# A written-out instruction order, and the engine of some casts and squares, replaced in a fused recurrence and MLP kernel

## The chip, the cores and the metric

The kernel runs on one core of a Trainium2 chip. Its time is the device time of one launch in microseconds; a kernel is told by the median over its runs. A profile is one further execution, taken by the hardware profiler, with a time of its own. TensorE is written PE, VectorE DVE, ScalarE ACT, GpSimd POOL and SyncE SP, as in the profile.

## What is computed

The first part is a linear recurrence over 768 steps for 4 batches and 8 heads of 48; the second is a two-layer MLP on its output.

```python
batch, n_heads, seq, head_dim = (4, 8, 768, 48)
n_tokens, d_model, d_ff = (3072, 384, 2048)
for t in range(S):
    cur = np.einsum('bhd,bhe->bhde', u[None] * kt, vt)
    y[:, :, t] = np.einsum('bhd,bhde->bhe', rt, state + cur)
    state = wt[:, :, :, None] * state + np.einsum('bhd,bhe->bhde', kt, vt)
x = attn_out.transpose(0, 2, 1, 3).reshape(B * S, H * D)
h = x @ w_in
r = np.maximum(h, 0.0)
g = s * (r * r) + b
return g @ w_out
```

## The kernel before

The recurrence is cut into 24 chunks of 128 time steps, numbered by `n`. A chunk has one operation of each of these names, most of them a single instruction or one group of matmuls. `load n.0` to `n.3` bring w, r, k and v (192 KB each; for chunks 0 to 3, two chunks are loaded together, 384 KB). `ln` takes the logarithm of w on ACT (line 317). `cum` sums it along time with triangular matrices on PE (L372, L391, with small column sums L380, L397); `exp` on ACT (L413), `inc` on DVE (L418) and `exn` on ACT (L428) turn the sums into decay factors, and `mul` on DVE (L437, L444) multiplies r and k by them. `tr` transposes both on PE (L471) and `tev` copies the result on ACT (L491, L494); from chunk 9 on, `tev` is a transposing DMA on SP's queue instead (L501). `mt` is the chunk's attention matrix on PE for a pair of chunks (L531, L543), `msk` its mask on DVE (two per chunk, L555), `vb` a cast of v to bf16 (L870 on ACT, L872 on POOL). `dmm` (L625, L638), `sup` (DVE, L671, L679) and `st` (POOL, L688) with `l2` (POOL, L458) carry the state to the next chunk of the same batch. `rkp`, `rku`, `yd` on POOL (L322, L328, L351) and `cd` on DVE (L345) make the term with u, which `u_mm` and `u_ev` (L893, L897) spread over the partitions. `ymm` gives the chunk's output on PE (L574, L586, L597, L606), `yev` takes it out on DVE (L651), `xtr` transposes it on PE (L699) and `xev` puts it into the MLP's input on ACT (L714).

The MLP works on 12 tiles `T` of two chunks, 256 tokens. `g1 T.i` (i = 0 to 7) is six matmuls of the first layer (L749), `relu T.i` its ACT pass (L762), `sq T.i` the square, on ACT (L772) or DVE (L774). `g2 T.q` is four matmuls of the second layer (L793): q = 0 to 3 for the tile's first 128 tokens, 4 to 7 for the other 128; the last tile has its second 128 tokens in two halves of the columns, 4 to 7 and 8 to 11. `oev T.k` scales and adds on DVE (L804), `store T.k` is the DMA to the output (L823). In the names of the order the tile's number and i or q are written together: `g211.4` is `g2` of tile 11, q = 4.

Early in the kernel `li0` to `li3` and `lo0` to `lo3` load the two weight matrices in pieces of 768 KB, `ci` and `co` cast them to bf16, and `csred`, `csadd`, `cssplit` (DVE), `csspread` (PE, L849) and `csevac` (ACT, L855) make the constant row that b and the column sums of `w_out` give. `small` and `small2` load s and b. `warm` matmuls (L1119, written `+16`) only use PE while it has nothing else.

No scheduler runs when the kernel is built. The order is written out by hand as one text, `ORDER`; each engine and each DMA queue gets its operations in the sequence in which the text names them, `@A`, `@D` or `@P` gives the engine where there is a choice, and every queue works strictly in that order. Waits come from data and from buffers that are used in a ring: an operation that takes a buffer must wait until its user of one round before is done.

```python
need = o["deps"] + o["after"]
for tag, last in o["takes"]:
    h = held[tag]
    if len(h) >= self.rings[tag]:
        need += h[-self.rings[tag]]
    h.append(last)
```

The rings that matter here are six PSUM banks `P` for nearly all PE results but those of `g2`, two PSUM banks `o` for `g2`, eight r/k buffers, five for w, six for v, four for the output rows and four for the weight pieces. The numbers in the `add(...)` calls are the planner's costs and due times from which an order was searched beforehand; they issue no instruction.

Of the kernel before, what the change touches and what calls it, by code (L numbers as in the profile page):

```python
# [38 lines left out]
load0.0 load0.1 load_u ln0 ln1 +16 cum0.0 cum0.1 cum1.0 exp0.0 load0.2 exp0.1 mul0.0 mul0.1 exp1.0  # L39
load0.3 mul1.0 cum1.1 load2.0 load2.2 load2.3 u_mm tr0 exp1.1 mul1.1 +2 tr1 u_ev tev0 tev1 +9 mt0  # L40
vb0@P load4.0 l20 rkp0 rku0 load2.1 rkp1 l21 msk0.0 msk1.0 vb1@A ln2 msk0.1 rku1 li0 ln3 cd0 +4
cum2.0 exp2.0 dmm0 cum3.0 msk1.1 cum3.1 ln4 vb2@A cum2.1 sup0 exp3.0 exp2.1 vb3@A st0 +1 cum4.0 li1
exp3.1 l22 yd0 mul2.0 mul2.1 exp4.0 mul3.0 ymm0 cd1 mul3.1 yd1 ymm1 dmm1 tr2 sup1 rkp2 l23 ci0@A
yev0 dmm2 tev2 tr3 li2 rku2 sup2 yev1 xtr0 tev3 cd2 +5 xtr1 l24 rkp3 xev0 rku3 yd2 xev1 +1 mt2 g10.0
ci1@A msk2.0 st2 msk2.1 msk3.0 li3 g10.1 relu0.1 msk3.1 relu0.0 dmm3 g10.2 g10.3 relu0.2 lo0 ymm2
ci2@D cd3 ymm3 lo1 st1 yd3 lo2 sup3 yev2 cum4.1 xtr2 ci3@A relu0.3 g10.4 load5.0 sq0.0@D lo3 load5.1
yev3 load6.0 load4.1 sq0.3@A g10.5 co0@D load4.2 xev2 xtr3 load5.2 csred0@D sq0.2@A sq0.1@A relu0.4
g10.6 xev3 exp4.1 small2 g20.4 g20.0 g10.7 load4.3 g11.0 g11.1 co1@D relu0.5 g11.2 sq0.5@A relu0.7
relu0.6 sq0.4@D sq0.7@A csred1@D sq0.6@A ln5 small g11.3 relu1.0 vb4@P load5.3 rkp4 csadd1@D relu1.2
relu1.3 g20.1 g11.4 cum5.0 relu1.1 exp5.0 co2@D csred2@D g20.5 cum5.1 exp5.1 sq1.2@A csadd2@D  # L50
# [113 lines left out]
def kernel(  # L164
# [15 lines left out]
    B, H, S, D = r.shape  # L180
# [979 lines left out]
```

## Time and profile before

| | us |
|---|---|
| median of 11 runs | 186.07 |
| lowest, highest run | 185.84, 189.53 |
| profiled execution, its own time | 186.16 |
| span of the profiled execution | 184.1 |
| PE, DVE, ACT, POOL busy | 176.5, 140.6, 146.5, 106.3 |
| `g1` and `g2` matmuls, busy (L749, L793) | 71.9, 72.7 |

The span runs from the first to the last instruction; 2.06 us of the profiled run's time lie outside it. A group's busy time is the time in which at least one of its instructions was running; since matmuls overlap, the mean of one is longer than its share. "Idle before" names the instruction whose end let the engine go on. A row of busy time by stage gives the stage, its length, the busy time of PE, PE's weight loads, DVE, ACT and POOL with the number of instructions in brackets, the granted share of PE's clock, the mean busy share of the DMA engines and the rate in GB/s.

### The profile page before, as it was taken

Reading aid. Unit: us, or ns where it says so; the run is one execution under the profiler, and the core shown is the slowest. Engines: PE = TensorE matmul, PEld = TensorE weight load, DVE = VectorE, ACT = ScalarE, POOL = GpSimd, SP = SyncE. Lnnn points to the kernel's source line nnn. Section 1 sums busy time; section 2 is a strip of 40 time slices with the busy share of each in tenths; the row PEclk is TensorE's granted clock in tenths of the full one; section 3 lists DMA queues with packets and bytes.
Section 4 is the critical chain, followed back from the end, with each engine's and each line's share of the span. In section 5 each row is a group of like instructions: output and inputs, shape, how many; then the busy total and the mean of one; then the engine's idle time right before and its main releaser. Section 6 shows DMA issues by size and latency. Waiting matters only on the chain.

```text
span 184.1 us, 5087 instructions
## 1 busy us (share of the span) xinstructions
PE 176.5 (96%) x1994; PEld 139.6 (76%) x1994; DVE 140.6 (76%) x250; ACT 146.5 (80%) x286; POOL 106.3 (58%) x139
## 2 busy tenths in 40 slices
PE   7999999998999999997999999999999999999993
PEld 4468898865797787785788878877886978888672
DVE  7659899999969878959978698697898959522231
ACT  3589999997889999888878979878989687754900
POOL 3684950049698999698397199195396493100000
PEclk9999999999999999999999999999999999999999
DMA  6999999879999769898799989999874890004022
GB/s 160 325 327 365 393 317 318 165 139 221 208 192 220 182 123 217 179 212 183 134 221 185 177 197 218 215 238 200 193 162 97 193 192 4 2 5 171 0 85 85
DMA packets 113449, 34.14 MB, mean 185 GB/s; under 512 B 108177, under 2 KB 111378, under 8 KB 113426
## 3 DMA queue, kind: packets, MB, share of 16 engines
q1 hardware_dynamic: 113426, 33.83, 79.3%
q8 instruction: 15, 0.25, 0.5%
q14 instruction: 8, 0.07, 0.1%
HBM read 25.17 MB, written 4.72 MB: 162 GB/s over the span
## 4 chain that ended last, share of the span: by engine, by line
PE 46%; ACT 3%; DVE 2%; issue 0%; ACTq 0%
PE o_ps L793 21%; PE h_ps L749 19%; PE mt_ps L543 2%; DVE mt_sb L555 2%; PE y_ps L606 1%; ACT rh L762 1%; PE xt_ps L699 1%; PE y_ps L597 1%; ACT gT L772 1%; PE d_ps L638 1%; PE cums L391 1%; DVE o_sb L804 1%; ACT E L428 0%; ACT xT L714 0%; DVE inc L418 0%; ACT E L413 0%
## 5 line engine op out<-in xcount | busy, mean ns | idle before, releaser
L793 PE MATMUL o_ps<-w_out,gT 128*128 128x384 bf16 (+1 forms) x400 | 72.7, 320 | 1.0 <-DVE o_sb L804 0.7
L749 PE MATMUL h_ps<-xT,w_in 128*128 128x256 bf16 x576 | 71.9, 273 | 0.2
L762 ACT ACTIVATE rh<-h_ps 128x512 bf16<-128x512 f32 x96 | 55.3, 601 | 13.9 <-PE h_ps L749 12.8
L749 PEld LDWEIGHTS <-w_in 128*128 128x128 bf16 x576 | 61.7, 114 | 4.3 <-issue 0.2
L793 PEld LDWEIGHTS <-gT 128*128 128x128 bf16 x400 | 36.5, 98 | 18.6 <-DVE gT L774 0.8
L772 ACT ACTIVATE gT<-rh 128x512 bf16<-128x512 bf16 x69 | 42.5, 636 | 0.3
L351 POOL TENSOR_TENSOR yd<-vt,cd 128x384 bf16<-128x384 f32 x20 | 19.0, 954 | 18.4 <-DVE cd L345 18.4
L555 DVE TENSOR_TENSOR mt_sb<-mt_ps,tri_strict 128x512 bf16<-128x512 f32 x40 | 25.4, 681 | 2.7 <-PE mt_ps L543 2.7
L328 POOL TENSOR_TENSOR rku<-rkp,u_bc 128x384 f32<-128x384 f32 x24 | 25.3, 1057 | 0.7
L322 POOL TENSOR_TENSOR rkp<-rkt 128x384 f32<-128x384 f32 x20 | 23.7, 1189 | 1.3 <-DMA rkt<-in_k_dram 1.3
L804 DVE SCALAR_TENSOR_TENSOR o_sb<-o_ps,s_bc,bconst 128x384 f32<-128x384 f32 (+1 forms) x25 | 14.8, 594 | 11.8 <-PE o_ps L793 11.8
L444 DVE TENSOR_TENSOR prd<-rkt,E 128x768 bf16<-128x768 f32 x20 | 23.2, 1164 | 0.5 <-ACT E L428 0.3
L774 DVE TENSOR_TENSOR gT<-rh 128x512 bf16<-128x512 bf16 x27 | 14.9, 562 | 9.2 <-ACT rh L762 9.1
L413 ACT ACTIVATE E<-cums 128x388 f32<-128x388 f32 (+1 forms) x32 | 15.8, 497 | 6.5 <-DVE inc L418 3.2
L688 POOL TENSOR_TENSOR st<-stmp,l 128x384 bf16<-128x384 bf16 x16 | 16.4, 1026 | 6.4 <-DVE stmp L679 6.4
L872 POOL CAST vb<-vt 128x384 bf16<-128x384 f32 x12 | 7.2, 603 | 16.1 <-DMA vt<-in_v_dram 16.1
L651 DVE TENSOR_TENSOR x_sb<-y_ps,yd 128x384 bf16<-128x384 f32 x24 | 13.0, 553 | 4.2 <-PE y_ps L606 2.2
L345 DVE TENSOR_REDUCE cd<-rku 128x8 f32<-128x384 f32 x24 | 12.9, 543 | 0.6 <-POOL rku L328 0.6
L714 ACT COPY xT<-xt_ps 128x384 bf16<-128x384 bf16 x24 | 11.0, 487 | 2.5 <-PE xt_ps L699 2.4
L418 DVE TENSOR_TENSOR inc<-cums,logw 128x384 f32<-128x384 f32 x16 | 8.8, 550 | 3.9 <-ACT E L413 3.4
L317 ACT ACTIVATE logw<-wt 128x384 bf16<-128x384 f32 x20 | 10.6, 531 | 0.0
L679 DVE TENSOR_TENSOR stmp<-d_ps,st 128x384 bf16<-128x384 f32 x16 | 8.7, 551 | 2.1 <-PE d_ps L638 2.0
(94 smaller groups left out, 199.4 us busy)
## 6 DMA issues: line engine op xcount, KB each, us to landing
out_dram<-o_sb SPq DMA_DIRECT2D x23, 192.0 KB, 3.3
wt<-in_w_dram SPq DMA_DIRECT2D x20, 192.0 KB, 3.9
rkt<-in_r_dram SPq DMA_DIRECT2D x20, 192.0 KB, 4.0
rkt<-in_k_dram SPq DMA_DIRECT2D x20, 192.0 KB, 3.8
vt<-in_v_dram SPq DMA_DIRECT2D x20, 192.0 KB, 3.6
wi_st<-in_moe_w_in_dram SPq DMA_DIRECT2D x4, 768.0 KB, 9.1
wo_st<-in_moe_w_out_dram SPq DMA_DIRECT2D x4, 768.0 KB, 5.8
pkt<-in_w_dram SPq DMA_DIRECT2D x2, 384.0 KB, 4.1
```

What stands on the lines that cost most here:

```text
L322: nc.gpsimd.tensor_tensor(out=rkp, in0=c["r"], in1=c["k"], op=ALU.mult)
L328: nc.gpsimd.tensor_tensor(out=rku.rearrange("t h d -> t (h d)"), in0=c["rkp"].rearrange("t h d -> t (h d)"), in1=u_bc, op=ALU.mult,)
L351: nc.gpsimd.tensor_tensor(out=yd, in0=c["v"], in1=c["cd"].unsqueeze(2).to_broadcast([128, H, D]), op=ALU.mult,)
L413: nc.scalar.activation(out=c["E"][:, x, 0:w], in_=ps[:, 0:w], func=AF.Exp)
L444: nc.vector.tensor_tensor(out=prd[:, :, :, 0:D], in0=c["rk"], in1=c["E"][:, :, 0:HD].rearrange("t x (h d) -> t x h d", h=H), op=ALU.mult,)
L555: nc.vector.tensor_tensor(out=c["mt"][:, sg], in0=c["mt_ps"][sg], in1=(masks[:, n % 2] if packed(n) else tri_strict) .unsqueeze(1) .to_bro ...
L688: nc.gpsimd.tensor_tensor(out=c["st_new"], in0=c["stmp"].rearrange("q p (g e) -> q p g e", g=2), in1=c["l2"].unsqueeze(3).to_broadcast([12 ...
L749: nc.tensor.matmul(ps[:, f, :], lhsT=w_in_sb[ft // FPP][:, kt, :].rearrange("p (m j) -> p j m", j=FPP)[:, ft % FPP, :], rhs=xT[T][:, kt, : ...
L762: nc.scalar.activation(out=rh, in_=hs[T, i], func=AF.Relu)
L772: nc.scalar.activation(out=g, in_=rh, func=AF.Square)
L793: nc.tensor.matmul(os_[T, k][:, cols], lhsT=gT[T][:, ft, tt * 128 : (tt + 1) * 128], rhs=w_out_sb[ft // FPP][:, ft % FPP, cols], start=(ft ...
L804: nc.vector.scalar_tensor_tensor(out=o_sb[:, cols], in0=os_.pop((T, k))[:, cols], scalar=s_bc, in1=bconst[:, cols], op0=ALU.mult, op1=ALU.add,
```

## The change

The text `ORDER` is replaced by another one of the same 1105 words, found by a search that took the mean over seven sets of disturbed durations. Nothing else that issues an instruction is different: the operations, the buffers and their rings, and the 38 warm-up matmuls are the same. The engines of ten casts of v and of 23 squares are exchanged; 11 casts are on ACT and 13 on POOL in both, 69 squares are on ACT before and 68 after. One of the planner's costs, that of `u_mm`, is 0.85 instead of 0.7. The diff is cut to the beginning, up to the first groups of tile 2, two later stretches and the end:

```diff
--- before
+++ after
 ORDER = """
-load0.0 load0.1 load_u ln0 ln1 +16 cum0.0 cum0.1 cum1.0 exp0.0 load0.2 exp0.1 mul0.0 mul0.1 exp1.0
-load0.3 mul1.0 cum1.1 load2.0 load2.2 load2.3 u_mm tr0 exp1.1 mul1.1 +2 tr1 u_ev tev0 tev1 +9 mt0
-vb0@P load4.0 l20 rkp0 rku0 load2.1 rkp1 l21 msk0.0 msk1.0 vb1@A ln2 msk0.1 rku1 li0 ln3 cd0 +4
-cum2.0 exp2.0 dmm0 cum3.0 msk1.1 cum3.1 ln4 vb2@A cum2.1 sup0 exp3.0 exp2.1 vb3@A st0 +1 cum4.0 li1
-exp3.1 l22 yd0 mul2.0 mul2.1 exp4.0 mul3.0 ymm0 cd1 mul3.1 yd1 ymm1 dmm1 tr2 sup1 rkp2 l23 ci0@A
-yev0 dmm2 tev2 tr3 li2 rku2 sup2 yev1 xtr0 tev3 cd2 +5 xtr1 l24 rkp3 xev0 rku3 yd2 xev1 +1 mt2 g10.0
-ci1@A msk2.0 st2 msk2.1 msk3.0 li3 g10.1 relu0.1 msk3.1 relu0.0 dmm3 g10.2 g10.3 relu0.2 lo0 ymm2
-ci2@D cd3 ymm3 lo1 st1 yd3 lo2 sup3 yev2 cum4.1 xtr2 ci3@A relu0.3 g10.4 load5.0 sq0.0@D lo3 load5.1
-yev3 load6.0 load4.1 sq0.3@A g10.5 co0@D load4.2 xev2 xtr3 load5.2 csred0@D sq0.2@A sq0.1@A relu0.4
-g10.6 xev3 exp4.1 small2 g20.4 g20.0 g10.7 load4.3 g11.0 g11.1 co1@D relu0.5 g11.2 sq0.5@A relu0.7
-relu0.6 sq0.4@D sq0.7@A csred1@D sq0.6@A ln5 small g11.3 relu1.0 vb4@P load5.3 rkp4 csadd1@D relu1.2
-relu1.3 g20.1 g11.4 cum5.0 relu1.1 exp5.0 co2@D csred2@D g20.5 cum5.1 exp5.1 sq1.2@A csadd2@D
-load6.1 load6.2 g11.5 co3@D sq1.0@D g11.6 csred3@D csadd3@D load7.0 cssplit g11.7 g20.2 g20.6 g20.3
-rku4 mul4 relu1.4 load8.0 sq1.3@A ln6 load9.0 relu1.6 relu1.7 sq1.1@A cum6.1 g20.7 relu1.5 csspread
-load6.3 mul5 tr4 cum6.0 load7.1 tr5 csevac sq1.5@A l25 oev0.1 oev0.0 exp6.0 tev5 exp6.1 dmm4 g21.4
-g21.0 tev4 g21.1 g21.5 vb5@P sup4 sq1.4@A cd4 dmm5 mul6 mt4 rkp5 load7.2 ln7 load7.3 g21.6 sup5
-msk4.0 msk5.0 sq1.6@A sq1.7@A cum7.0 rku5 st5 l26 ln8 exp7.0 msk4.1 tr6 g21.2 yd4 tev6 load10.0
-load8.3 cd5 cum7.1 yd5 ymm4 msk5.1 g21.7 st4 yev4 load8.1 ln9 vb6@P exp7.1 load8.2 ymm5 yev5 cum8.0
-inc8 xtr4 mul7 load9.1 load9.3 cum9.0 xev4 dmm6 xtr5 st3 g21.3 l27 xev5 exp8.0 load11.0 vb7@P g12.0
-rkp7 sup6 exn8 load10.1 g12.1 inc9 exp9.0 oev1.1 relu2.0 sq2.0@A g12.2 relu2.1 dmm7 tr7 rku7 g12.3
-tev7 relu2.2 rkp6 sq2.1@D oev1.0 load11.3 vb8@P cd7 sup7 mul8 load9.2 g12.4 g22.0 relu2.3 relu2.4
...
-g14.1 g14.2 g14.3 cd10 relu4.0 exp13.0 inc13 sup11 mul12 l212 cd11 oev3.0 relu4.1 yd10 vb12@P mt10
-relu4.2 g14.4 g23.7 relu4.3 sq4.0@D sq4.1@A load13.3 load14.1 exn13 st10 load13.2 msk10.0 msk11.0
-load15.0 oev3.1 rkp12 l213 msk10.1 relu4.4 ln14 g14.5 store2.0 load16.0 g24.4 st11 msk11.1 sq4.2@A
-cum14.0 g24.0 dmm12 rku12 sq4.4@A g14.6 yd11 sup12 mul13 ymm10 ymm11 yev10 ln15 rkp13 relu4.5
...
-relu7.7 sq7.7@A store5.1 relu8.0 mt18 tev20 exn21 msk19.0 relu8.1 msk18.0 msk18.1 yd19 g27.6 g18.2
-ln22 msk19.1 g18.3 cum22.0 dmm18 g27.2 sq8.1@A ln23 inc22 mul21 g27.3 ymm19 g18.4 g27.7 relu8.3
-relu8.2 rkp20 sq8.0@A load22.2 g18.5 tev21 sq8.3@A yev19 relu8.4 exp22.0 rku20 yd18 vb21@P rkp21
-sup18 relu8.5 ymm18 xtr19 rku21 st18 sq8.2@A exn22 cum23.0 sq8.4@D g18.6 oev7.1 yev18 oev7.0 xtr18
-g18.7 g28.0 inc23 store7.0 relu8.6 g28.4 load20.3 g28.5 cd21 xev18 exp23.0 xev19 supn21 supn20
-sq8.5@A relu8.7 load23.2 mt20 store6.1 g19.0 mul22 g19.1 g28.1 msk20.0 msk20.1 msk21.0 yd21 msk21.1
...
-xev23 relu10.6 relu10.7 oev9.0 sq10.4@D g111.0 g111.1 g29.7 g111.2 sq10.5@D relu11.1 g210.4 sq10.7@A
-g111.3 g111.4 relu11.0 g111.5 oev9.1 sq10.6@D sq11.1@D g111.6 relu11.5 g111.7 relu11.2 sq11.5@A
-relu11.3 sq11.2@A sq11.0@A relu11.6 store9.1 g210.5 relu11.7 g210.0 g210.6 g210.7 store8.1 store9.0
-g210.1 relu11.4 sq11.3@A g210.2 store8.0 sq11.6@D sq11.7@D oev10.1 g210.3 sq11.4@D g211.8 g211.0
-g211.1 oev10.0 store10.1 g211.2 g211.4 g211.3 g211.5 g211.6 g211.7 g211.9 g211.10 g211.11 oev11.0
-oev11.1 oev11.2 store10.0 store11.1 store11.0 store11.2
-"""
+load0.0 ln0 load0.2 load0.1 ln1 +17 cum0.0 cum0.1 exp0.0 mul0.0 cum1.0 cum1.1 exp0.1 exp1.0 mul0.1
++3 tr0 load0.3 l21 exp1.1 mul1.0 mul1.1 vb0@A l20 vb1@A load_u u_mm rkp0 tr1 dmm0 u_ev load2.0
+load4.0 tev0 tev1 sup0 ln2 rku0 load2.1 st0 cd0 rkp1 ln3 +5 mt0 +1 cum2.0 cum2.1 load2.3 load2.2
+msk0.0 li0 cum3.0 ln4 vb3@A msk1.0 exp2.0 vb2@A msk0.1 li2 +1 cum4.0 exp3.0 msk1.1 yd0 mul2.0 cum3.1
+rku1 exp2.1 exp3.1 mul2.1 cd1 l22 mul3.0 ymm0 ci0@A ymm1 li1 yev0 exp4.0 tr2 dmm1 yd1 mul3.1 +8 xtr0
+rkp3 li3 tev2 yev1 rku3 sup1 xev0 st1 tr3 rkp2 ci2@D xtr1 xev1 dmm2 sup2 lo0 tev3 load5.0 +3 g10.0
+ci1@A mt2 msk3.0 relu0.0 lo1 g10.1 g10.2 msk2.0 msk2.1 sq0.0@A relu0.1 msk3.1 rku2 ci3@A g10.3 g10.4
+st2 relu0.4 relu0.2 l23 l24 ymm3 cd3 sq0.1@D yd3 ymm2 lo2 cd2 lo3 yev3 xtr3 small2 yd2 co0@D g10.5
+relu0.3 sq0.2@A sq0.4@A ln5 yev2 relu0.5 g10.6 xtr2 g20.4 xev2 csred0@D xev3 load6.0 load4.1 load4.2
+load5.1 sq0.3@A load5.2 relu0.6 cum5.0 g10.7 co1@D sq0.5@A load6.1 csred1@D csadd1@D co2@D g11.0
+g20.0 relu0.7 exp5.0 sq0.7@A relu1.0 g11.1 csred2@D cum5.1 exp5.1 sq0.6@A g20.1 g11.2 g11.3 cum4.1
+g20.5 co3@D small relu1.3 relu1.2 relu1.1 sq1.0@A load7.0 csadd2@D load6.2 ln6 load4.3 load5.3 g20.6
+g11.4 csred3@D g11.5 relu1.4 g20.2 exp4.1 csadd3@D load6.3 sq1.3@A g20.3 cum6.0 relu1.5 g20.7
+cssplit sq1.1@A mul4 csspread sq1.2@D csevac g11.6 exp6.0 relu1.6 cum6.1 mul5 tr4 dmm3 exp6.1 l26
+g11.7 tev4 tr5 oev0.1 tev5 sup3 relu1.7 sq1.4@A oev0.0 g21.0 g21.1 rkp4 mt4 rkp5 g21.4 vb4@P mul6
+msk5.0 sq1.5@A sq1.7@A rku4 rku5 msk4.0 load8.0 l25 msk4.1 tr6 cd4 dmm4 load9.0 sup4 yd4 load7.1 st4
+load7.2 sq1.6@A vb5@A cd5 ln7 vb6@A tev6 load7.3 msk5.1 load8.1 ln8 g21.5 g21.2 g21.6 load8.2 dmm5
+cum7.0 exp7.0 yd5 ymm4 g21.7 sup5 yev4 ymm5 cum7.1 xtr4 cum8.0 yev5 inc8 load9.3 load10.0 load9.1
+ln9 dmm6 rkp6 st3 l27 exp7.1 load11.0 load8.3 xev4 vb7@P xtr5 xev5 cum9.0 exp8.0 mul7 load9.2 sup6
+g21.3 exn8 g12.0 exp9.0 g12.1 rkp7 rku6 relu2.0 tr7 g12.2 relu2.1 inc9 st5 oev1.1 oev1.0 sq2.1@A
+rku7 g12.3 dmm7 tev7 relu2.2 sq2.0@D relu2.3 g12.4 sup7 mul8 cd6 rkp8 relu2.4 g12.5 g22.4 mt6
...
+g23.2 dmm10 cd10 g14.0 sup10 exn12 relu4.0 rku11 load13.3 mt10 g23.6 g14.1 sq3.7@A msk10.0 msk10.1
+msk11.0 cum13.0 g14.2 g14.3 store1.1 load13.1 msk11.1 inc13 mul12 cd11 load13.2 load14.0 relu4.1
+ymm10 relu4.2 sq4.0@D exp13.0 rkp12 store2.1 relu4.3 exn13 g23.3 g23.7 yd10 load16.0 load15.0
+load14.1 sq4.1@A ymm11 g14.4 load14.3 oev3.1 yd11 rkp13 g24.0 g14.5 st11 rku12 g14.6 load14.2
+sq4.2@A sq4.3@A ln14 relu4.4 load15.1 l212 relu4.5 mul13 relu4.6 yev11 load12.3 oev3.0 yev10 rku13
...
+sq8.6@A mt18 g28.2 g28.4 yd19 g28.5 load21.3 msk19.0 load22.1 msk19.1 msk18.0 sq8.7@A exn22 rkp21
+store6.1 ymm19 g28.6 cum23.0 exp23.0 rku21 load22.2 msk18.1 yev19 ymm18 cd21 xtr19 yev18 rku20 inc23
+g28.3 xtr18 g28.7 vb20@P xev18 xev19 mt20 supn20 cd20 msk20.0 g19.0 g19.1 vb21@P yd20 msk20.1 g19.2
...
+g210.3 g111.4 relu11.2 relu11.3 g111.5 g111.6 sq11.1@D sq11.0@D sq11.2@D oev10.0 relu11.5 g111.7
+relu11.4 sq11.4@A sq11.3@D relu11.7 g210.7 relu11.6 g211.0 g211.1 sq11.7@D sq11.6@D oev10.1 sq11.5@A
+g211.8 g211.4 store10.0 g211.5 store10.1 g211.2 g211.9 g211.3 g211.6 oev11.0 g211.7 oev11.1 g211.10
+store11.0 g211.11 oev11.2 store11.1 store11.2
 """
...
 add("load_u", "SP", 0.5, load_u, (), [], [], U_AT, dma=0.1)
-add("u_mm", "PE", 0.7, spread_u, (), ["load_u"], [("o", ["u_ev"])], 2.0, lat=0.2)
+add("u_mm", "PE", 0.85, spread_u, (), ["load_u"], [("o", ["u_ev"])], 2.0, lat=0.2)
 add("u_ev", "DVE", 0.45, u_evac, (), ["u_mm"], [], 2.0)
```

## The prediction

> **What bounds the kernel now.** I read the page first, then busy time by stage, then the waits of TensorE and ScalarE, then TensorE's timeline where it waits.
>
> ```profile
> span 184.1 us, 5087 instructions
> PE 176.5 (96%) x1994; PEld 139.6 (76%) x1994; DVE 140.6 (76%) x250; ACT 146.5 (80%) x286; POOL 106.3 (58%) x139
> PEclk9999999999999999999999999999999999999999
> ```
>
> TensorE (PE) is busy in 96% of the span and its clock is granted throughout, so what an order can save is TensorE idle time and slack at the two ends. By stage (us, then busy us of PE, PEld, DVE, ACT, POOL):
>
> ```profile
> 0.00:21.00 21.00, 19.12 (x292) 13.26 (x293) 15.41 (x41) 15.00 (x26) 13.55 (x33) 1.00 1.00 308
> 21.00:51.80 30.80, 29.65 (x352) 23.48 (x352) 29.31 (x46) 28.09 (x52) 15.13 (x18) 1.00 0.98 237
> 51.80:170.00 118.20, 116.81 (x1269) 95.11 (x1268) 92.06 (x157) 98.42 (x201) 77.64 (x90) 1.00 0.79 165
> ```
>
> The reader sees three regimes. Up to 21 us the pipeline fills. From 21 to 51.8 three engines are nearly full at once: PE idles 1.15, DVE 1.49, ACT 2.71 us. From there to 170 us PE idles only 118.20 - 116.81 = 1.39 us. TensorE's waits, first for 20 to 52 us, then for 52 to 181 us:
>
> ```profile
> PE trps L471 <- DVE prd L444: 1.2, 2, 0.8
> ```
>
> ```profile
> PE o_ps L793 <- DVE o_sb L804: 0.7, 1, 0.7
> PE o_ps L793 <- DVE gT L774: 0.3, 1, 0.3
> PE xt_ps L699 <- ACT E L428: 0.3, 1, 0.3
> ```
>
> The timeline places them: both transposes of chunks 4 and 5 late behind `mul4`, `mul5`; `g24.4` and `g24.0` late behind a DVE burst of masks; one `xtr` late behind an exponential.
>
> ```profile
> 41.01 0.62 PE L471 MATMUL trps<-identity,prd 128*128 128x128 bf16 x8 [0.34 <-DVE prd L444]
> 42.68 0.62 PE L471 MATMUL trps<-identity,prd 128*128 128x128 bf16 x8 [0.81 <-DVE prd L444]
> 84.30 0.82 PE L793 MATMUL o_ps<-w_out,gT 128*128 128x384 bf16 x4 [0.33 <-DVE gT L774]
> 86.02 0.81 PE L793 MATMUL o_ps<-w_out,gT 128*128 128x384 bf16 x4 [0.66 <-DVE o_sb L804]
> 139.78 0.34 PE L699 MATMUL xt_ps<-identity,x_sb 128*128 128x128 bf16 x3 [0.32 <-ACT E L428]
> ```
>
> A rule weighed here: the Trainium skill, "Perfetto Trace Analysis", section "Identifying the Most-Contended Engine", says that matmul busy share is no measure of headroom and to judge by weight-load busy share and MFU. By weight loads, 95.11 of 118.20 us, the long stage would have 23 us of room. The rows say otherwise for an order: in the chain six `g1` matmuls take 0.66 us and four `g2` matmuls 0.65, group after group, 109 and 163 ns each with no gap. I take the row: 1.4 us of room there, not 23.
>
> **The change, part by part.** No instruction is added or dropped on TensorE (3987 rows each, 38 warm-up matmuls in both). `u_mm` 0.7 to 0.85 is a planner's number that issues nothing: 0. The 24 casts of v stay 11 on ACT and 13 on POOL, with other members, and of 96 squares 68 instead of 69 are on ACT. One square is 0.52 us of ACT (two back to back, 1.15 us busy and the next begins 1.04 after) and about 0.4 of DVE; both have over 35 us idle in the span, so the totals are 0. What counts is where each queue's work stands. I compare at points where TensorE has issued the same set of work in both orders, so that its time is directly comparable. Two exist early: the end of `tr5` (43.14 us before) and the start of `g12.0` (51.79).
>
> Start to `g10.0` (20.94 before). `vb0` goes from POOL to ACT and stands with `vb1` ahead of `tev0`. ACT waits 0.90 us there before, and two casts of 0.43 fill it; `mt0` stays at 11.1. `dmm0` and `sup0` move ahead of the masks, and `u_mm` (0.85) behind `tr0`, covered by `tev0`. The four masks then end near 14.1 and `ymm0` starts there, not at 15.1. But `g10.0` also waits for `ci0` (its 768 KB load stands behind the same loads as before) and for `xev1`: 16.5 + 1.4 cast, 0.4 `exp4.0`, 0.95 `tev2`, 0.8 two `xev` = 20.1. `tev3` (0.95) and then `mt2` come after it, not before it. Gain 0.8, returned by `mt2`: 21.7 after `mt2` and `g10.0` against 21.6. Sum 0.
>
> To `tr5`. Before, `tr4` follows `csspread` at once and waits out `mul4`, `mul5` (1.46 us each, DVE rows from 39.69 to 42.62). After, `g11.6`, `cum6.1` (0.66 + 0.16) stand between `csspread` and `tr4`, and `dmm3`, `g11.7` (0.44 + 0.66) between `tr4` and `tr5`: 1.9 us of work in front of the wait. But DVE has done less: up to `cssplit` it drops three squares and `sup3` and takes one square, 1.2 us less, while PE up to `csspread` does 1.7 us less. So half a microsecond of the cover is spent on `csspread` itself. On POOL, `rkp4`, `rkp5` now precede `vb4`, whose load 4.3 falls from sixteenth to twentieth on SP's queue from `li0` on, past 6.1, 7.0, 6.2 and the slow 512 B load `small` (2.20 us on SP). It is issued near 39.5 instead of 35.15 (2.2, and three loads of about 0.7) and lands 3.6 later, near 43; `dmm4`, its first user, comes near 45, so 0, but a further 2 us would reach TensorE.
>
> The second rule: "GPSIMD Engine Reference" (its opening table, SBUF interfaces) says that POOL shares them with VectorE and that DVE instructions with two SBUF inputs contend. That speaks against this move, because `rkp4`, `rkp5` now run beside `csred3`, `csadd3`. The rows agree on size: `rkp` takes 1.71 us beside `mul4`, 1.00 alone, and `mul` 1.46 against 0.95. By the rule alone `tr5` loses about 0.5; but POOL then sits waiting for load 4.3 while `mul4`, `mul5` run, and they lose 2 x 0.5. Net DVE: `cssplit` 39.7, `mul4` 40.65, square 41.05, `mul5` 42.0, `tr5` ends 42.6 at best and 43.0 if the muls keep 1.46. I take a gain of 0.3 of the 1.15.
>
> To `g12.0`. ACT must finish `xev5`. Its queue up to there gains `vb0`, `vb5`, `vb6` (3 x 0.43) and `sq0.0`, `sq0.4`, `sq1.0` (3 x 0.52) and loses `sq0.1`, `sq1.2` (2 x 0.52): +1.8 us. These are its waits from 16 to 52 us:
>
> ```profile
> ACT RK L494 <- PE trps L471: 0.9, 1, 0.9
> ACT xT L714 <- PE xt_ps L699: 0.5, 1, 0.5
> ACT bconst L855 <- PE csb_ps L849: 0.3, 1, 0.3
> ACT rh L762 <- PE h_ps L749: 0.2, 1, 0.2
> ```
>
> With 0.2 more and the 0.90 before `tev0`, 3.0 us are there to fill. From `tev5` (end 43.6 to 44.0) 7.4 us of queue follow to `xev5`, with 0.3 of small waits 51.3 to 51.7. TensorE, at the same work, would arrive at 51.5. So `g12.0` gains 0.3; bounds +1.8 (nothing filled) and -0.7.
>
> 51.8 us to the end. Of 1.39 us idle, 0.99 is at `g24.4` and `g24.0`. Before, 2.8 us of PE work lie between `mt10` and `g24.0`; after, 5.6 (`g23.6`, `g14.1`, `g14.2`, `g14.3`, `ymm10`, `g23.3`, `g23.7`, `ymm11`, `g14.4`, `cum13.0`). DVE must by then do four masks, `inc13`, `mul12`, `cd11`, one square, `oev3.1`: 4 x 0.61 + 0.47 + 0.95 + 0.47 + 0.41 + 0.53 = 5.3. So 0.9 to 0.6 of it goes. The 0.32 at `xtr18` goes with its neighbours. What is late next: `ymm18` 3.1 us behind `mt18` (four masks, 2.5), and `mt20`, `g19.0` behind `inc23` and `xev19` with a few tenths of cover. I give new waits 0.8 in all, from 0.3 to 2.0, for 118 us that I can't follow wait by wait; the old order has 1.39. The tail does not move: both orders end in two half groups of 0.33, the 0.42 `o_sb` and a store.
>
> Sum: 0 - 0.3 - 1.4 + 0.8 = -0.9. The profiled run took 186.16 with a span of 184.1; the median shown is 186.07. Span 183.2, time 185.2.
>
> **The rivals.**
> 1. ACT turns late (slower). Place: `g12.0` behind `xev5`. ACT has 1.8 us more to do by then and runs full for 28 us in a row. It decides once ACT idles over about 1 us between `relu0.0` and `xev5`, by a late `ci1`, `ci3`, `tr5` or load 4.3. If the cover is gone, +1.8, then -1.4 and the same mechanism's later waits of +0.9: 187.4. For it: ACT already has 28.09 of 30.80 us busy. Against: each old wait is one that the new order puts work into.
> 2. Waits only change places (no change): no gain at `g12.0`, 1.4 of new waits for 1.4 old: 186.1. For it: every wait of the long stage is under 0.7 us, so small misplacements make as many.
> 3. Everything is covered: -0.7 at `g12.0` and 0.3 of new waits for 1.4: 184.3. Against: the masks of `mt18` and `mt20`.
>
> **How the numbers follow.** Likeliest case (185.2, own range 184.7 to 185.5) 0.33, rival 3 0.09, rival 2 0.23, rival 1 0.35. A measurement of this kernel tells about 0.3%, 0.56 us, from no change. Faster 0.42, same 0.23, slower 0.35. Range 184.0 (rival 3's lower side) to 188.2 (rival 1 with 2 instead of 0.9 of later waits, less its tail).
>
> **What would show it.** Right: `tr4`, `tr5` with under 0.6 us of wait together; `g12.0` near 51.5; ACT nearly without waits from 22 to 51; under 0.5 us at `g24.0`; long-stage PE idle under 1 us. Wrong: PE waiting for ACT's `xT` at `g12.0`; `dmm4` waiting for `vb4`; TensorE idle over 1.5 us after 52, above all near `mt18` to `g19.0`, or a transpose on SP late ahead of an `mt`.

## Result, and the profile after

| | before | after |
|---|---|---|
| median, us | 186.18 (48 runs) | 184.05 (13 runs) |
| ratio of comparable runs | | 0.9899, 95% interval 0.9877 to 0.9920 |
| profiled execution, its own time, us | 186.16 | 183.94 |
| span, us | 184.1 | 182.2 |

Medians are of all runs; ratios leave out runs more than 1.5% above the fastest of the same kernel. The change makes the kernel 1% faster: 2.1 us in the median where 0.9 was predicted. The time lies in the range given (184.0 to 188.2), but below the own range of the likeliest case (184.7 to 185.5). It is what rival 3, "everything is covered", stood for (184.3).

The page after. TensorE has the same busy time in a shorter span:

```profile
span 182.2 us, 5106 instructions
PE 176.5 (97%) x1994; PEld 139.8 (77%) x1994; DVE 144.2 (79%) x251; ACT 145.5 (80%) x285; POOL 103.8 (57%) x139
```

Busy time by stage, the columns as before (length, then busy PE, PEld, DVE, ACT, POOL; clock; DMA share; GB/s):

```profile
0.00:21.00 21.00, 19.39 (x264) 13.26 (x265) 15.78 (x40) 15.03 (x26) 14.10 (x31) 1.00 0.99 301
21.00:51.80 30.80, 30.66 (x387) 24.09 (x386) 28.99 (x47) 29.93 (x57) 14.29 (x20) 1.00 0.99 249
51.80:170.00 118.20, 117.83 (x1273) 95.38 (x1271) 95.63 (x159) 97.32 (x197) 75.43 (x90) 1.00 0.81 164
```

TensorE's idle time fell from 1.15 to 30.80 - 30.66 = 0.14 us in the second stage and from 1.39 to 118.20 - 117.83 = 0.37 in the third. ACT went from 28.09 to 29.93 busy of 30.80: the 1.8 us of casts and squares that the new order gives it went into its old idle time.

TensorE's waits from 52 us on were three lines, 1.3 us in all. Now there is one:

```profile
PE xt_ps L699 <- DVE x_sb L651: 0.3, 1, 0.3
```

TensorE's timeline, the rows that answer to the late transposes of before and the start of `g12.0`. None of them has a releaser behind it, so none waits:

```profile
40.36 0.61 PE L471 MATMUL trps<-identity,prd 128*128 128x128 bf16 x8
42.03 0.61 PE L471 MATMUL trps<-identity,prd 128*128 128x128 bf16 x8
51.11 1.47 PE L749 MATMUL h_ps<-xT,w_in 128*128 128x256 bf16 x12
```

The points at which both orders have issued the same set of TensorE work place the gain (us; each is the start of what follows, the 115th operation is taken 0.65 us behind the start of its last group, and TensorE's end is the end of its last row):

| point | before | after | difference |
|---|---|---|---|
| end of `mt2` and `g10.0` | 21.60 | 21.85 | +0.25 |
| end of `tr5` | 43.14 | 42.47 | -0.67 |
| start of `g12.0` | 51.79 | 51.11 | -0.68 |
| 115th operation (`g22.3` after, `g13.5` before) | 70.08 | 69.15 | -0.93 |
| end of TensorE | 180.87 | 178.66 | -2.21 |

These are one profile of each kernel. A second profile of the kernel after (`after_again`, below) has 21.95, 42.71, 51.34 and 178.92 at four of these points, so a difference is good to some 0.3 us. 0.3 us is given back behind TensorE, in the last `o_sb` and stores (3.5 us from TensorE's end to the end of the span, 3.2 before), and the time outside the span is 1.74 instead of 2.06.

### The profile page after: what moved, and what is told of

It is laid out like the page before. It is cut to its first block, busy times and chain, and to the rows that moved or that the text cites. A ratio compares the mean times of both kernels' runs of the same rounds, so it can differ in the third digit from the quotient of the medians.

```text
span 182.2 us, 5106 instructions
## 1 busy us (share of the span) xinstructions
PE 176.5 (97%) x1994; PEld 139.8 (77%) x1994; DVE 144.2 (79%) x251; ACT 145.5 (80%) x285; POOL 103.8 (57%) x139
## 4 chain that ended last, share of the span: by engine, by line
PE 84%; SPq 6%; DMA 5%; DVE 2%; ACT 1%; issue 1%; DVEq 0%
PE o_ps L793 34%; PE h_ps L749 33%; DMA wi_st<-in_moe_w_in_dram 5%; SPq L304 4%; PE mt_ps L543 3%; PE y_ps L606 2%; PE xt_ps L699 2%; PE cums L391 2%; PE y_ps L597 2%; PE d_ps L638 2%; PE trps L471 1%; SPq L719 1%; DVE prd L444 1%; ACT w_in L870 1%; PE y_ps L586 1%
## 5 line engine op out<-in xcount | busy, mean ns | idle before, releaser
L749 PE MATMUL h_ps<-xT,w_in 128*128 128x256 bf16 x576 | 72.9, 273 | 0.1
L762 ACT ACTIVATE rh<-h_ps 128x512 bf16<-128x512 f32 x96 | 54.8, 601 | 15.1 <-PE h_ps L749 14.4
L772 ACT ACTIVATE gT<-rh 128x512 bf16<-128x512 bf16 x68 | 41.5, 639 | 0.3
L351 POOL TENSOR_TENSOR yd<-vt,cd 128x384 bf16<-128x384 f32 x20 | 17.7, 886 | 24.1 <-DVE cd L345 17.5
L774 DVE TENSOR_TENSOR gT<-rh 128x512 bf16<-128x512 bf16 x28 | 15.7, 575 | 12.1 <-ACT rh L762 12.0
L444 DVE TENSOR_TENSOR prd<-rkt,E 128x768 bf16<-128x768 f32 x20 | 24.1, 1208 | 0.1
L322 POOL TENSOR_TENSOR rkp<-rkt 128x384 f32<-128x384 f32 x20 | 21.0, 1054 | 1.9 <-DMA rkt<-in_k_dram 1.9
L458 POOL TENSOR_TENSOR l<-E,par 128x8 f32<-128x8 f32 x20 | 6.0, 306 | 20.0 <-ACT E L413 20.0
```

Source lines behind the costliest of these rows:

```text
L322: nc.gpsimd.tensor_tensor(out=rkp, in0=c["r"], in1=c["k"], op=ALU.mult)
L351: nc.gpsimd.tensor_tensor(out=yd, in0=c["v"], in1=c["cd"].unsqueeze(2).to_broadcast([128, H, D]), op=ALU.mult,)
L444: nc.vector.tensor_tensor(out=prd[:, :, :, 0:D], in0=c["rk"], in1=c["E"][:, :, 0:HD].rearrange("t x (h d) -> t x h d", h=H), op=ALU.mult,)
L749: nc.tensor.matmul(ps[:, f, :], lhsT=w_in_sb[ft // FPP][:, kt, :].rearrange("p (m j) -> p j m", j=FPP)[:, ft % FPP, :], rhs=xT[T][:, kt, : ...
L762: nc.scalar.activation(out=rh, in_=hs[T, i], func=AF.Relu)
L772: nc.scalar.activation(out=g, in_=rh, func=AF.Square)
```

## The experiments

Ratios are to before on the same chip, with 95% intervals. In the profiles of the other five kernels with the old first part, ACT waits for the first weight piece and casts it 1.0 to 1.7 us later than in the profile of before; positions in them are therefore read against a point near by.

**1. The two halves alone.** `head` takes the new order up to `g12.0` and the rest in the old one; `tail` the other way round (with `inc9` ahead of `g12.1`).

```diff
 head:  (new) ... mul7 load9.2 sup6 g21.3 exn8 g12.0
-exp9.0 g12.1 rkp7 rku6 relu2.0 tr7 g12.2 ... (rest of the new order)
+st5 rkp7 load10.1 g12.1 inc9 exp9.0 ... (what is left, in the old order)
```

> The new order up to g12.0, the old order for what is left. Theory, gains add by stage: g12.0 starts near 51.1 us instead of 51.8, the old waits at g24.4, g24.0 and at xtr18 stay (about 1.3 us of TensorE idle from 52 to 170 us), the ratio to before is near 0.9965. Rival, the lead is lost: later stages are held by loads, DVE or ACT, the 0.7 us come back as waits after 52 us and the ratio is 1.000 within 0.001.

> The old order up to g12.0, the new one for what is left (inc9 moved ahead of g12.2, which the ring of PSUM banks asks for). Theory, gains add by stage: tr4 and tr5 wait as before, g12.0 near 51.8, TensorE idle from 52 to 170 us under 0.6 us, ratio near 0.993. Rival, the new second part needs the state in which the new first part leaves ACT (1.8 us more done by g12.0): ACT waits appear from 52 to 75 us and the ratio is 0.997 or more.

`head`: 185.91 us, ratio 0.9992 (0.9961 to 1.0023): no difference, the rival's case. `tail`: 185.41, ratio 0.9938 (0.9904 to 0.9972): the theory's. In `head`'s profile `g12.0` starts at 51.24, 0.55 earlier than before, but `mt8` at 70.73 against 70.82. TensorE's old waits stand where they were:

```profile
84.22 0.82 PE L793 MATMUL o_ps<-w_out,gT 128*128 128x384 bf16 x4 [0.33 <-DVE gT L774]
85.94 0.81 PE L793 MATMUL o_ps<-w_out,gT 128*128 128x384 bf16 x4 [0.66 <-DVE o_sb L804]
```

TensorE gives the lead back between 55 and 61 us. DVE gives its own back there too: `mul8` starts 0.4 earlier than before but takes 1.33 instead of 0.94, so the masks behind it start at 58.20 in both. `head`:

```profile
56.94 1.33 DVE L444 TENSOR_TENSOR prd<-rkt,E 128x768 bf16<-128x768 f32 x1
58.20 1.27 DVE L555 TENSOR_TENSOR mt_sb<-mt_ps,tri_strict 128x512 bf16<-128x512 f32 x2
```

and before:

```profile
57.34 0.94 DVE L444 TENSOR_TENSOR prd<-rkt,E 128x768 bf16<-128x768 f32 x1
58.20 1.28 DVE L555 TENSOR_TENSOR mt_sb<-mt_ps,tri_strict 128x512 bf16<-128x512 f32 x2
```

So a lead of half a microsecond was worth nothing by itself here: the next stage was not laid out to use it. That DVE alone holds TensorE there is argued from these rows, not shown. `tail`'s profile is of an execution of 189.6 us in which `g12.0` starts only at 56.69; it has 0.39 us of TensorE idle from 51.8 to 170 us, and none of the old waits from `g12.0` on. The two ratios multiply to 0.993; whether the whole (0.990) is more than that, the intervals don't tell.

**2. Order without engines, engines without order.** `order_only` has the new sequence with the old engine of every cast and square; `eng_only` the old sequence with the new ones, for example

```diff
 order_only: -vb0@A  +vb0@P    -vb5@A +vb5@P   -sq0.4@A +sq0.4@D
 eng_only:   -vb0@P  +vb0@A    -vb5@P +vb5@A   -sq0.4@D +sq0.4@A
```

> The new order with the old engine for each cast and square. Theory, the order carries the gain: tr4 and tr5 still without a wait, ratio 0.990 to 0.993. Rival, the engine choice carries at least half: with three squares back on DVE ahead of cssplit (0.4 us each) csspread, tr4 and tr5 come 0.7 us later, g12.0 with them, and the ratio is 0.995 or more.

> The old order with the new engine for each cast and square. Theory, the order carries the gain: no more than 0.3 us either way, ratio 0.998 to 1.002. Rival, ACT has 1.8 us more to do before xev5 in an order that was not laid out for it: xev5 and g12.0 come up to 1.5 us later, ratio 1.004 to 1.008.

`order_only`: 187.22, ratio 1.0068 (1.0048 to 1.0088). From 51.8 to 170 us its TensorE idles only 0.41 us, as after; what it loses lies ahead of that. `g12.0` starts at 52.91, 1.8 us later than after, with these new waits on the way:

```profile
40.55 0.32 PE L849 MATMUL csb_ps<-cs_sum,ones 128*128 128x384 bf16 x1 [0.27 <-DVE cs_sum L842]
49.45 0.33 PE L638 MATMUL d_ps<-vb,prd 128*128 128x96 bf16 x4 [0.47 <-POOL vb L872]
```

DVE gets its squares back and is late for `csspread`; POOL gets `vb5` back and is late for `dmm5`. That names 0.74 of the 1.8 us; 0.28 more is there already behind `mt2` and `g10.0`. `eng_only`: 191.29, ratio 1.0282 (1.025 to 1.0314). Its transposes wait 1.7 us, not 1.15, and `g2` groups that did not wait before do, 1.1 us of it at 30.93 for one square. TensorE's granted clock also falls in this profile (last section), but the three runs with a clock of 0.999 or 1.00 took 190.68 to 191.42 us too. The transposes:

```profile
43.68 0.62 PE L471 MATMUL trps<-identity,prd 128*128 128x128 bf16 x8 [0.89 <-DVE prd L444]
45.35 0.76 PE L471 MATMUL trps<-identity,prd 128*128 128x128 bf16 x8 [0.81 <-DVE prd L444]
```

Order and engines are one plan: either half alone is slower than before.

**3. One old wait, taken out by itself.** `b_oev` is the order before with one word moved:

```diff
-sq4.0@D sq4.1@A ... msk10.0 msk11.0 load15.0 oev3.1 rkp12
+sq4.0@D oev3.1 sq4.1@A ... msk10.0 msk11.0 load15.0 rkp12
```

> The order before, with oev3.1 put on DVE ahead of the masks of chunks 10 and 11. Theory (the gain of the later part is the sum of its old waits, one by one): the 0.66 us at g24.0 goes, nothing new of over 0.2 us appears, median 185.5, ratio 0.997. Rival (a wait moved is not a wait removed: the masks are 0.53 us later and ymm10 or g24.4 waits in its place): PE idle from 52 to 170 us stays at 1.3 to 1.5, median 186.1 to 186.3.

185.9 us, ratio 0.9958 (0.9928 to 0.9989): the theory. `o_sb` is now read out before the four masks (DVE), and `g24.0` starts without a wait (PE):

```profile
84.01 0.60 DVE L804 SCALAR_TENSOR_TENSOR o_sb<-o_ps,s_bc,bconst 128x384 f32<-128x384 f32 x1
84.54 2.47 DVE L555 TENSOR_TENSOR mt_sb<-mt_ps,tri_strict 128x512 bf16<-128x512 f32 x4
```

```profile
84.14 0.82 PE L793 MATMUL o_ps<-w_out,gT 128*128 128x384 bf16 x4 [0.33 <-DVE gT L774]
85.07 0.81 PE L793 MATMUL o_ps<-w_out,gT 128*128 128x384 bf16 x4
```

The profile begins with a late weight piece (`mt2` at 20.83 instead of 20.17), but `tr4` and `tr5` then wait only 0.31 us, so that the delay is gone by 84 us: an old wait was also slack. TensorE's lead on before grows from 0.16 us at 84.14 to 0.95 at 85.07, and the span is 0.8 shorter: with the masks 0.5 later nothing else waits. The wait shown as 0.66 us was worth 0.8. A row of matmuls ends some 0.16 us behind the moment at which the next row can start, so idle time between rows shows less than a wait costs: counted from start to start, the wait at `g24.0` is 0.80 us. That the other waits are worth their length too was not tested one by one.

**4. POOL's place beside DVE.** The prediction let `rkp4`, `rkp5` run beside the column sums. After, they don't, because `l26` stands ahead of them on POOL and waits for `exp6.0`:

```profile
40.86 0.60 POOL L458 TENSOR_TENSOR l<-E,par 128x8 f32<-128x8 f32 x1 [14.16 <-ACT E L413]
41.42 1.96 POOL L322 TENSOR_TENSOR rkp<-rkt 128x384 f32<-128x384 f32 x2
```

so that DVE runs its chain to `mul5` next to an idle POOL:

```profile
38.77 0.56 DVE L842 TENSOR_TENSOR cs_sum<-wo_st,cs_sum 128x384 bf16<-128x384 f32 x1
39.24 0.95 DVE L444 TENSOR_TENSOR prd<-rkt,E 128x768 bf16<-128x768 f32 x1
40.11 0.42 DVE L774 TENSOR_TENSOR gT<-rh 128x512 bf16<-128x512 bf16 x1
40.45 0.95 DVE L444 TENSOR_TENSOR prd<-rkt,E 128x768 bf16<-128x768 f32 x1
```

`pool_early` is the order after with the two words where I had thought them:

```diff
-mul5 tr4 dmm3 exp6.1 l26 g11.7 ... g21.1 rkp4 mt4 rkp5 g21.4
+mul5 tr4 dmm3 exp6.1 rkp4 rkp5 l26 g11.7 ... g21.1 mt4 g21.4
```

> The order after, with rkp4 and rkp5 ahead of l26 on POOL, where the prediction had thought them; nothing else moves. In the profile of after l26 stands ahead of them and holds POOL for exp6.0 until 40.86, so that csred3 to cssplit and mul4 run with POOL at rest. Theory (POOL beside DVE was the term that I mis-sized): both rkp now start before 39 us, csred3, csadd3 or cssplit take up to 0.5 us longer together, cssplit ends near 39.8 instead of 39.33, tr5 ends 0.3 to 0.5 us later than 42.47 and g12.0 starts at 51.2 to 51.5; median 184.1 to 184.6, ratio to before about 0.990. Rival (the early gain has nothing to do with POOL's place, since exp6.0 and the drop of three squares alone give it): cssplit within 0.1 us of 39.33, g12.0 at 51.1, median 184.05.

185.64 us, ratio 0.9949 (0.9910 to 0.9988): half of the gain is gone. POOL's two `rkp` take their usual 1.0 us; DVE pays (POOL, then DVE of this kernel):

```profile
33.94 1.00 POOL L322 TENSOR_TENSOR rkp<-rkt 128x384 f32<-128x384 f32 x1 [7.52 <-DMA rkt<-in_k_dram]
35.95 1.12 POOL L322 TENSOR_TENSOR rkp<-rkt 128x384 f32<-128x384 f32 x1 [1.02 <-DMA rkt<-in_k_dram]
```

```profile
33.11 2.23 DVE L831 TENSOR_TENSOR wo_st<-wo_st 128x768 f32<-128x768 f32 x2
36.14 1.35 DVE L838 TENSOR_TENSOR wo_st<-wo_st 128x384 f32<-128x384 f32 x1
```

After, the same two rows take 1.55 and 0.55: 0.68 + 0.80 = 1.5 us more for DVE. `csspread` pays nearly all of it,

```profile
39.99 0.32 PE L849 MATMUL csb_ps<-cs_sum,ones 128*128 128x384 bf16 x1 [1.14 <-DVE cs_sum L841]
40.59 0.32 PE L849 MATMUL csb_ps<-cs_sum,ones 128*128 128x384 bf16 x1 [0.27 <-DVE cs_sum L842]
```

and `g12.0` comes 1.2 us later than after, the span is 1.2 longer. I expected 0.3 to 0.5: right in kind, less than half in size. `tr5` ends at 43.68 here, 0.5 us later than before the change.

Before, POOL and DVE do meet, in `rkp4` and the two `mul` (POOL, then DVE):

```profile
40.10 1.71 POOL L322 TENSOR_TENSOR rkp<-rkt 128x384 f32<-128x384 f32 x1
```

```profile
39.69 2.93 DVE L444 TENSOR_TENSOR prd<-rkt,E 128x768 bf16<-128x768 f32 x2
```

`b_pool_late` tries the same cure on this order: `l26` behind `exp6.0`, `rkp4` and `rku4` behind it.

```diff
-vb4@P load5.3 rkp4 csadd1@D ... rku4 mul4 ... exp6.0 tev5 ... st5 l26
+vb4@P load5.3 csadd1@D ... mul4 ... exp6.0 l26 rkp4 rku4 tev5 ... st5
```

> The order before, with l26 put right behind exp6.0 on its engines' queues and rkp4 and rku4 behind it, so that POOL is at rest while mul4 and mul5 run. Theory: mul4 and mul5 take 0.95 instead of 1.46 us each, the waits of tr4 and tr5 (0.34 and 0.81) all but vanish, and g12.0 starts 0.3 to 0.7 us before 51.79; how much reaches the end depends on what follows, as the lead of 0.55 us at g12.0 was lost by mt8 with the old rest; median 185.6 to 186.2. Rival (mul is slow for a reason other than POOL): mul4 and mul5 keep 1.46, waits as before, 186.18.

187.72 us, ratio 1.0093 (1.0045 to 1.0141): slower, which neither theory had. Four of the twelve runs, the profiled one among them, have a granted clock of 0.988 to 0.991 and 189.4 to 189.7 us; the median of the other eight is 187.26, 0.9 above that of before on the same chip. From 40 to 56 us, where the rows below stand, the clock of the profile is 1.00. The profile has the intended effect, both muls together 1.82 us instead of 2.93,

```profile
42.91 1.82 DVE L444 TENSOR_TENSOR prd<-rkt,E 128x768 bf16<-128x768 f32 x2
```

and from `csspread` to the end of `tr5` TensorE needs 2.14 us, 0.8 less than before. But `rku4` now ends after 47 us, and DVE stands for it at `cd4`, with the masks and the state queued behind:

```profile
47.70 0.55 DVE L345 TENSOR_REDUCE cd<-rku 128x8 f32<-128x384 f32 x1 [1.46 <-POOL rku L328]
```

That reaches TensorE:

```profile
50.41 0.61 PE L471 MATMUL trps<-identity,prd 128*128 128x128 bf16 x8 [0.36 <-DVE st L671]
52.20 0.35 PE L606 MATMUL y_ps<-vb,mt_sb 128*128 128x48 bf16 x7 [0.36 <-DVE mt_sb L555]
```

`tr5` to `g12.0` takes 55.24 - 45.24 = 10.0 us instead of 8.65. The cure cost more than the contention: 1.35 us against 0.8. In the order after `rku4` is as late (its row begins 2.06 us behind the end of `tr5`, here 1.43), but there `mul6` and three masks stand ahead of `cd4` on DVE.

**5. How much room ACT has.** Five passes of Square over 128x256 into a scratch tile, added behind `tev5` after, behind `csevac` before:

```diff
+    def extra(i):
+        nc.scalar.activation(out=xout, in_=warm_sb, func=AF.Square)
+    for i in range(5):
+        add(("xa", i), "ACT", 0.5, extra, (i,), [], [], 0.0)
-oev0.1 tev5 sup3
+oev0.1 tev5 xa0 xa1 xa2 xa3 xa4 sup3
```

> The order after with work added: five more passes of Square over a 128 by 256 tile into a scratch tile on ACT, right behind tev5, some 1.6 to 2 us of ACT in all; the output is not touched. It measures how much room ACT has before g12.0. Theory of rival 1 of the prediction (ACT is the next limit there, and the room is what was idle, under 0.3 us): g12.0 starts 1.3 to 1.7 us later than 51.11 behind xev5, and nearly all of it reaches the end, 185.3 to 186. Theory that ACT has slack (its waits before g12.0 are small because its work is in order, not because it is full): under 0.5 us at g12.0, under 184.6 at the end.

> The order before, with the same five extra passes of Square on ACT (1.9 us of ACT, output not touched) behind csevac, ahead of the 0.89 us that ACT waits for tr5 and the 0.54 us for xtr4. Theory (before had idle ACT time there, and the new order has spent it on casts and squares): the first 1.4 us are swallowed, g12.0 starts 0.4 to 0.7 us after 51.79 against the 1.4 us that the same work cost the order after; median 186.5 to 187. Rival (the waits of ACT were no room, since what follows them is as late whatever comes before): g12.0 1.4 to 1.9 us later, median 187.6 to 188.

`act_load`: 185.88 us, ratio 0.9969 (0.9935 to 1.0003), span 183.7. ACT's next `relu` starts at 45.49 instead of 43.58, 1.9 us later, and TensorE stalls for a square and a cast of ACT's:

```profile
46.65 1.67 PE L793 MATMUL o_ps<-w_out,gT 128*128 128x384 bf16 x8 [0.34 <-ACT gT L772]
48.60 0.33 PE L638 MATMUL d_ps<-vb,prd 128*128 128x96 bf16 x4 [0.28 <-ACT vb L870]
```

with smaller gaps behind them. From the end of `tr5` to the start of the last `g2` stretch it is 174.18 - 42.27 = 131.9 us against 172.61 - 42.47 = 130.1 after. `tr5` ends 0.2 earlier here and the last stretch starts 1.57 later: 1.8 of 1.9 us reach the end. After has next to no room on ACT there.

`b_act_load`: 188.32 us, ratio 1.0101 (1.0039 to 1.0162). Its profile is of an execution of 190.06 us, whose clock was down to 0.50 at 24 to 26 us and is 1.00 from 28 us on. Up to `g12.0` the theory looks right: from the start of `csevac` to the end of `xev5` ACT needs 11.6 us instead of 11.0, so two thirds of the work fell into old waits, and 0.25 is left of the 0.54 us at `xT`:

```profile
54.45 1.09 ACT L714 COPY xT<-xt_ps 128x384 bf16<-128x384 bf16 x2 [0.25 <-PE xt_ps L699]
```

Yet the ratio stands for 1.9 us (0.7 to 3.0), the rival's figure. But the runs are wide apart: three took 187.19 to 187.66 us, the others 188.97 to 190.06. They don't decide between the two, and where the rest is lost stays open.

**6. A tighter start.** `start` is the order after with

```diff
-load0.0 ln0 load0.2 load0.1 ... li2 ... li1 ... +8 xtr0 ... ci2@D xtr1 xev1 dmm2 sup2 ... +3 g10.0
+load0.0 load0.1 ln0 load0.2 ... li1 ... li2 ... +2 xtr0 ... xtr1 xev1 dmm2 sup2 ci2@D ... +1 g10.0
```

and `after_again` is the kernel after, run beside it.

> The order after with its first 22 us tightened, in the hope of a faster kernel: li1 ahead of li2, load0.1 ahead of load0.2, ci2 on DVE behind sup2, and only 2 and 1 warm-up matmuls instead of 8 and 3 ahead of xtr0 and g10.0. Theory (ACT's wait of 0.52 us for xtr0 and the 0.65 us that ci2 holds DVE waiting for li2 are paid by TensorE): g10.0 starts 0.3 to 0.6 us before 20.51, nothing later gives it back, since TensorE has no idle of over 0.1 us from there to 74 us; median 0.3 to 0.6 us below that of the order after on the same chip. Rival (the loads of the weights pace this stretch: ci0 already waits 0.83 us for li0, and the pieces come no sooner): g10.0, g10.1 or g10.2 waits for a cast of w_in instead, tr5 ends at 42.4 as before, no difference.

> The order after, unchanged, beside the other two on the same chip, as their measure. Every theory: ratio to before 0.988 to 0.992, tr5 ends near 42.5, g12.0 near 51.1.

`start`: 185.12 us, ratio 0.9922 (0.9889 to 0.9955); `after_again`: 184.20, ratio 0.9889 (0.9846 to 0.9932). The rival's mechanism: TensorE does reach `g10.0` earlier, and only waits longer. `start`, then `after_again`:

```profile
20.43 0.82 PE L749 MATMUL h_ps<-xT,w_in 128*128 128x256 bf16 x6 [1.70 <-ACT xT L714]
```

```profile
20.46 0.82 PE L749 MATMUL h_ps<-xT,w_in 128*128 128x256 bf16 x6 [0.96 <-ACT xT L714]
```

ACT stands in front of that with `ci0`, which waits for the first weight piece, 2.05 us in `start`, 1.54 in `after_again`:

```profile
16.85 1.47 ACT L870 CAST w_in<-wi_st 128x1536 bf16<-128x1536 f32 x1 [2.05 <-DMA wi_st<-in_moe_w_in_dram]
```

`tr5` ends at 42.74 and 42.71, and the spans are 182.5 and 182.4. In these two profiles the landing of that 768 KB load sets the pace up to 21 us.

The median of `start` is nevertheless 0.9 us longer, which neither theory had. Six of its twelve runs have a mean granted clock of 0.987 to 0.991 and 184.90 to 185.83 us; the other six have 1.00 and a median of 184.43. None of the six runs of `after_again` is under 0.997. `start` has eight warm-up matmuls fewer and a longer wait at `g10.0`; which of its edits lets the clock fall was not tested apart. None of the kernels here beats the order after.

## Why the prediction was right, and why by too little

The mechanism was right: TensorE's total stays (the page counts 1994 matmuls and 1994 weight loads in both kernels, one row more than the prediction), its holes are filled by order, and every hole named went. Rival 3, "everything is covered", had both of its terms right, 0.7 us at `g12.0` (0.68 measured) and 0.3 of new idle time (0.37), and was given a chance of only 0.09. Of the prediction's steps:

1. *Start to `g10.0`, 0.* Measured +0.25: after `mt2` and `g10.0` TensorE stands at 21.85 against 21.60 (21.7 was worked out). The returned gain of `ymm0` was right (14.50 instead of 15.1). What I missed is that the stretch can be paced by the first weight piece, as in the profiles of `start` and `after_again`.
2. *To `tr5`, -0.3.* Measured -0.67. This step failed in size, and the term is the 0.5 us of contention on `csred3`, `csadd3`, from which `cssplit` at 39.7 followed. It ended at 39.33, `mul5` at 41.40 instead of 42.0, and the transposes waited for nothing. I took the position of `rkp4`, `rkp5` ahead of `vb4` and overlooked `l26` ahead of both. The rule of the Trainium skill ("GPSIMD Engine Reference", opening table, SBUF interfaces: DVE instructions with two SBUF inputs contend with POOL) was right in kind, and `pool_early` shows that it is no small thing: where the two do meet, 1.2 us at `g12.0`. So two errors met in this step, a wrong place for POOL and too small a price for the meeting, and its good sign was luck: with POOL where I put it, `tr5` ends 0.5 us later than before, not 0.3 earlier. That `pool_early` has the ratio which I predicted (0.9949; 185.2 of 186.07 is 0.9953) is chance.
3. *To `g12.0`, -0.3.* Measured -0.68, the same lead as at `tr5`. ACT's queue was sized well: `tev5` ends at 43.68 (43.6 to 44.0), `xev5` 7.2 us later (7.4), and the start is TensorE's. Load 4.3 and `dmm4` cost nothing, as said. These are ACT's waits from 16 to 52 us after:

```profile
ACT w_in L870 <- DMA wi_st<-in_moe_w_in_dram: 0.8, 1, 0.8
ACT xT L714 <- PE xt_ps L699: 0.5, 1, 0.5
ACT bconst L855 <- PE csb_ps L849: 0.4, 1, 0.4
ACT E L413 <- PE h_ps L749: 0.3, 1, 0.3
```

   From `csevac` to `g12.0` ACT waits for nothing, where before had 0.89 and 0.54.
4. *52 us to the end, -1.4 + 0.8.* From `g12.0` to TensorE's end the gain is 1.53 instead of 0.6; this is the largest miss. The idle shown in the stage fell by 1.02, to 0.37. The sum itself took the whole old idle time, 1.4, although its working let only 0.6 to 0.9 of the 0.99 at `g24.4`, `g24.0` go; that hole went whole. The masks of chunk 18, `mt20` and `g19.0` turned out covered. The rest is in how a wait is counted. Six `g1` matmuls take 0.66 us from start to start, the four small column sums of a `cum` (L397) 0.10 and the three matmuls of an `xtr` 0.17, though their rows are longer. Rows of before, then of after:

```profile
83.15 0.82 PE L749 MATMUL h_ps<-xT,w_in 128*128 128x256 bf16 x6
85.12 0.24 PE L397 MATMUL cums<-ones,logw 128*128 128x1 bf16 x4
101.10 3.03 PE L749 MATMUL h_ps<-xT,w_in 128*128 128x256 bf16 x24
138.64 0.82 PE L749 MATMUL h_ps<-xT,w_in 128*128 128x256 bf16 x6
```

```profile
74.16 0.24 PE L397 MATMUL cums<-ones,logw 128*128 128x1 bf16 x4
85.36 0.33 PE L699 MATMUL xt_ps<-identity,x_sb 128*128 128x128 bf16 x3
```

   The rows that follow start at 84.30, 86.02, 103.97 and 139.78 before, at 74.67 and 85.80 after. That is 0.49 + 0.80 + 0.25 + 0.48 = 2.0 us too late before, one of them inside a row and not seen as idle, and 0.41 + 0.27 = 0.7 after: 1.3 of the 1.53. So the mis-sized term is the old waits, worth 2.0 and not 1.4; the new ones, 0.7, are near the 0.8 that I gave. What is left, 0.2 us, lies in steps of 0.1 or less.
5. *Tail, 0.* 0.3 was given back behind TensorE, and 0.3 won outside the span.

Rival 1 (ACT turns late) did not come about, but its mechanism is real: `act_load` shows that the order after is within 0.1 to 0.2 us of it at `tev5`. The new order used ACT's room up. Rival 2 (waits change places) is what `head`, `order_only` and `b_pool_late` did: each is an incomplete version of this change, and each fell back to before or behind it. The change as a whole did not; a forecast made from its order alone, or from its engines alone, would have had the wrong sign. Weighing the waits rather than the weight-load share was the right side for a change of order: the gain of the long stage, 1.5 us, is of the size of its waits, not of the 23 us that the share left.

## What to carry to other kernels

When TensorE is busy 96% of the span, add up its waits stage by stage, from the start of one row to the start of the next: that is what an order can win, and a single wait can be worth its full length (`b_oev`). Take an engine out from beside DVE's critical chain only after asking who waits for that engine's result, and read the whole queue in front of a moved instruction, also the words that the diff leaves unchanged. A lead pays only if the next stage is ordered to use it, and an order is tied to its engine assignment: test such a change whole.

## What the hardware showed that was not expected

- POOL and DVE do not share the loss evenly. In `pool_early` `rkp` took its usual 1.00 and 1.12 us, while DVE's two-input additions beside it took 0.68 and 0.80 us longer; in the profile of before both sides stretched (`rkp` 1.71, `mul` 1.46). There the two `mul` take 2.93 us, about what both and the `rkp` would take one after the other (2 x 0.95 + 1.00 = 2.90).
- TensorE's granted clock fell to about half behind short waits, but not behind each. In `eng_only`, behind the waits of 0.89 and 0.81 us at 43 to 45 us, it was 0.50 from 46 to 48 us and 0.73 to 50 (columns as in the stages above), and 16 `g2` matmuls took 4.18 us instead of 2.76. In the profiles of `tail`, `b_pool_late` and `b_act_load` it was 0.53, 0.50 and 0.50 from 24 to 26 us, behind waits of 1.71, 1.80 and 1.82 us at `mt2`. In `start`, a wait of 1.70 at nearly the same place left it at 1.00; so did 1.11 us at 30.93 in `eng_only`, and 0.34 and 0.81 in before. So such a wait can cost twice, and not each time.

```profile
46.00:48.00 2.00, 2.00 (x12) 1.13 (x10) 1.78 (x4) 1.85 (x3) 1.91 (x4) 0.50 1.26 217
48.00:50.00 2.00, 2.00 (x11) 1.03 (x9) 1.20 (x1) 2.00 (x5) 0.39 (x1) 0.73 1.16 206
```

- The cast of the first 768 KB piece of `w_in` begins anywhere from 15.45 to 17.06 us in the seven profiles with the new first part, and from 16.49 to 18.20 in the six with the old one.
